# Down product of parts for 36 chunks instead of 15, with some high parts on GpSimd, in a fused attention and SwiGLU kernel

## The chip, the cores and the metric

The kernel runs on one core of one Trainium2 chip. The metric is the device time of one execution in microseconds (us), as the median of several runs. Beside it there is one profiled execution, whose span and instructions the views below come from. The engines are TensorE (PE for its matmuls, PEld for its weight loads), VectorE (DVE), ScalarE (ACT), GpSimd (POOL) and SyncE (SP), which here only issues DMAs.

## The reference

Two stages are computed one after the other. First an attention with sketched polynomial features (4 batches, 4 heads, 1088 tokens, head size 32), then a feed-forward block on its 4352 x 128 result.

```python
def _attn_ref(q, k, v, S1, S2):
    def phi(x):
        a = np.einsum('rd,bhsd->bhsr', S1, x)
        b = np.einsum('rd,bhsd->bhsr', S2, x)
        return np.einsum('bhsi,bhsj->bhsij', a, b).reshape(*x.shape[:-1], r * r)
    q_p, k_p = (phi(q), phi(k))
    kv = np.einsum('bhsf,bhsd->bhfd', k_p, v)
    z = np.sum(k_p, axis=2)
    num = np.einsum('bhsf,bhfd->bhsd', q_p, kv)
    den = np.einsum('bhsf,bhf->bhs', q_p, z)[..., None] + 1e-06
    return num / den

def _moe_ref(x, w_gate, w_val, w_out):
    g = x @ w_gate
    silu = g * (1.0 / (1.0 + np.exp(-g)))
    val = x @ w_val
    return silu * val @ w_out
```

The widths are 128 (model) and 1536 (hidden). The change touches only the last product, `@ w_out`, called the down product here.

## The kernel before

The hidden width is worked on in 12 chunks of 128. The tokens are worked on in ten blocks: three of batch 0 (384, 384 and 320 tokens), which run as soon as their attention is there, and then seven of at most 480 tokens, which form the list `line` (numbered 0 to 6 in this text; 480 tokens each, the last 384). One unit is one chunk of one block. The seven blocks of `line` make 84 units, numbered y = 12 * block + chunk, and a single loop (L1355) runs over them. The attention of batches 1 to 3 is a generator, `attentions`, which that loop advances between the units (`group`, `parts_of`). All of it is one hand-written order: a manual schedule keeps instructions on each engine as they are written.

**A unit.** The gate and value products of the units in `line` are computed from parts in the type float32r: instead of one fp32 product with both factors whole, the factors are cut into a rounded high part, a rest, and a difference of scaled ones, and three float32r matmuls make up the product. `start_unit` issues the matmuls of the differences (L977, two of them, into a pair of PSUM banks) and ScalarE scales them in place (L980). One turn later `finish_unit` adds the other four matmuls (L990, L991), then ScalarE takes the SiLU (L993), and VectorE multiplies it with the value half into a slot of `hbuf` (L998). That releases the pair of PSUM banks; there are three pairs, so a later `start_unit` waits for it.

**The down product.** `down` takes the oldest chunk from the list `todo` once per turn, when over five wait there: the chunk of unit y is used about five turns later. A plain chunk is one fp32 matmul (L1062), which appears in the trace as two passes. For the pairs in `DOWN` the product is made of parts instead: `FINE` holds five chunks (1, 4, 6, 8, 10) and `DOWN` holds them for blocks 3 to 5 of `line`, 15 chunks in all. Such a chunk has three float32r matmuls (L1054, L1056, L1057), two of which sum in a PSUM bank of their own, `acc[i, "p"]`. When the block's last chunk of parts is done, `copy_out` lets ScalarE copy that bank (L1077), and after the block's last chunk `put_together` lets VectorE add both sums (L1083). Plain chunks in such a block use weights scaled beforehand (`scaled`), so that both sums fit.

**The parts.** `cut_hidden` is called at the end of `finish_unit(y)` for a chunk in `DOWN`. It puts off three operations to later turns: the high part h1 by ScalarE behind `finish_unit(y + 1)` (L954), the rest h0 by GpSimd in turn y + 2 (L955), and the scaled difference hd by VectorE in turn y + 3, ahead of that turn's L998 (L958). The results lie in three sets of three buffers, taken in turn (`h_sets`), in memory that the attention has left. `cut_down` makes the same parts of the down weights `wo`, as a generator that the loop advances at y = 24, 26, ..., 36 (L1371): high parts by ScalarE (L923), rests by GpSimd (L926), scaled rests by ScalarE (L931), differences by GpSimd (L934), and the scaled plain weights by ScalarE (L940). `cut_tokens` does the same for the tokens of the next block (L882 on ScalarE, L883 on GpSimd, L887 on VectorE).

```python
        add_to(behind, y + 1, lambda: nc.scalar.activation(h1, h, AF.Copy, scale=CUT))
        add_to(before, y + 2, lambda: nc.gpsimd.tensor_tensor(
            out=h0, in0=h, in1=whole(h1), op=ALU.subtract
        ))
        add_to(before, y + 3, lambda: nc.vector.scalar_tensor_tensor(
            out=hd, in0=whole(h0), scalar=-BETA, in1=whole(h1), op0=ALU.mult, op1=ALU.add
        ))
```

Of the kernel before, what the change touches and what calls it, by code (L numbers as in the profile page):

```python
# [7 lines left out]
FP32 = mybir.dt.float32  # L8
F32R = mybir.dt.float32r
# [3 lines left out]
AF = mybir.ActivationFunctionType  # L13
ALU = mybir.AluOpType
# [5 lines left out]
def kernel(  # L20
# [28 lines left out]
    nc = tc.nc  # L49
    P = nc.NUM_PARTITIONS  # L50
    B, H, S, Dh = q.shape
    R = S1.shape[0]
    D, Dff = moe_w_gate.shape
# [5 lines left out]
    NCH = Dff // P  # L59
# [11 lines left out]
    WB = 480  # L71
# [9 lines left out]
    const = ctx.enter_context(tc.tile_pool(name="const", bufs=1))  # L81
    stage = ctx.enter_context(tc.tile_pool(name="stage", bufs=2))
    apool = ctx.enter_context(tc.tile_pool(name="attn", bufs=1))
# [29 lines left out]
    def bank(tag=None):  # L113

        if tag is not None:
            i = place[tag]
        elif oldest[0]:
            i = min((i for i in used if i not in held), key=used.get)
        else:
            i = place[free_banks[turn[0] % len(free_banks)]]  # L120
            turn[0] += 1
        touch(i)
        return PS[:, i, :]
# [31 lines left out]
    wo = const.tile([P, NCH, D], FP32, name="wo")  # L155
# [32 lines left out]
    def load_next():  # L188
# [36 lines left out]
        out=ident[:], in_=ident[:], pattern=[[-1, P]], base=0, channel_multiplier=1,  # L225
# [90 lines left out]
    late = const.tile([P, NL, BW], FP32, tag="late", name="late", bufs=1)  # L316
# [500 lines left out]
    BETA = 4096.0  # L817
    CUT = 1.0 - 2.0**-13
# [3 lines left out]
    def whole(ap):  # L822
        return ap.bitcast(FP32)
# [17 lines left out]
    def cut_weights(w, lows, engine):  # L841

        rows = [], [], [], []
        sub = dict(op=ALU.subtract)
        for c, (w1, wb, wd) in enumerate(homes(w)):
            src = w[:, 3 * c : 3 * c + 3, :]
            low = lows[c]
            w_parts[id(w), c] = (w1, wb, wd)
            fine = dict(out=wd, in0=whole(w1), in1=whole(wb), **sub), engine.tensor_tensor
            if engine is nc.vector:  # L850
                fine = dict(
                    out=wd, in0=low, scalar=-BETA, in1=whole(w1), op0=ALU.mult, op1=ALU.add
                ), engine.scalar_tensor_tensor
            for row, f, args in zip(
                rows,
                (nc.scalar.activation, engine.tensor_tensor, nc.scalar.activation, fine[1]),
                (
                    dict(out=w1, in_=src, func=AF.Copy, scale=CUT),
                    dict(out=low, in0=src, in1=whole(w1), **sub),
                    dict(out=wb, in_=low, func=AF.Copy, scale=BETA),  # L860
                    fine[0],
                ),
            ):
                row.append((f, args))
        return rows
# [26 lines left out]


    line = list(range(HEAD, len(blocks)))
    FINE, PLAIN = (1, 4, 6, 8, 10), (0, 2, 3, 5, 7, 9, 11)
    DOWN = [(i, j) for i in line[3:6] for j in FINE]
    down_parts = {}
    h_parts = {}
    h_sets = []
    before, behind = {}, {}  # L900

    def add_to(where, y, f):
        where.setdefault(y, []).append(f)

    def now(where, y):
        for f in where.pop(y, ()):
            f()

    def cut_down():

        n = len(FINE)
        parts = const.tile([P, 3, n, D], F32R, tag="late", name="dparts", bufs=1)
        w1, wb, wd = (parts[:, k] for k in range(3))
        scaled = apool.tile([P, len(PLAIN), D], FP32, tag="zs", name="scaled")
        low = [
            apool.tile([P, c, D], FP32, tag=tag, name="low" + tag)[:]
            for tag, c in (("kas", 2), ("kab2", 3))
        ]
        down_parts.update(w1=w1, wb=wb, wd=wd, scaled=scaled)
        cs = slice(0, 2), slice(2, 5)  # L920
        runs = [(0, slice(1, 5, 3)), (2, slice(6, 11, 2))]
        for k, c in runs:
            nc.scalar.activation(w1[:, cs[k > 0]], wo[:, c, :], AF.Copy, scale=CUT)  # L923
        yield
        for (k, c), x in zip(runs, low):
            nc.gpsimd.tensor_tensor(  # L926
                out=x, in0=wo[:, c, :], in1=whole(w1[:, cs[k > 0]]), op=ALU.subtract
            )
            yield
        for c, x in zip(cs, low):  # L930
            nc.scalar.activation(wb[:, c], x, AF.Copy, scale=BETA)  # L931
        yield
        for c in cs:
            nc.gpsimd.tensor_tensor(  # L934
                out=wd[:, c], in0=whole(w1[:, c]), in1=whole(wb[:, c]), op=ALU.subtract
            )
            yield
        for k, c in ((0, slice(0, 1)), (1, slice(2, 4)), (3, slice(5, 12, 2))):
            m = len(range(12)[c])
            nc.scalar.activation(scaled[:, k : k + m, :], wo[:, c, :], AF.Copy, scale=-BETA)  # L940

    def cut_hidden(y, i, j):

        if not h_sets:
            x = []
            for tag in ("kld", "qld", "vld", "kT", "qT"):
                t = const.tile([P, 2, WB], F32R, tag=tag, name="h" + tag, bufs=1)
                x += [t[:, k, :] for k in range(2)]
            h_sets.extend(x[k : k + 3] for k in range(0, 9, 3))
        n = blocks[i][1]  # L950
        h_sets.append(h_sets.pop(0))
        h1, h0, hd = h_parts[i, j] = [x[:, 0:n] for x in h_sets[-1]]
        h = hidden[i, j][:, 0:n]
        add_to(behind, y + 1, lambda: nc.scalar.activation(h1, h, AF.Copy, scale=CUT))  # L954
        add_to(before, y + 2, lambda: nc.gpsimd.tensor_tensor(  # L955
            out=h0, in0=h, in1=whole(h1), op=ALU.subtract
        ))
        add_to(before, y + 3, lambda: nc.vector.scalar_tensor_tensor(  # L958
            out=hd, in0=whole(h0), scalar=-BETA, in1=whole(h1), op0=ALU.mult, op1=ALU.add
        ))  # L960


    room = const.tile([P, 10, BW], FP32, tag="room", name="room", bufs=1)
# [18 lines left out]
    def finish_unit(y):  # L982
        i, j = line[y // NCH], y % NCH
        n = blocks[i][1]
        x1, x0, _ = (x[:, 0:n] for x in x_parts[i])
        ps = sums_of.pop(y)
        now(before, y)
        for k, w in enumerate((wg, wv)):
            w1, wb = (w_parts[id(w), j // 3][t][:, j % 3, :] for t in range(2))
            nc.tensor.matmul(ps[:, k], w1, x1, start=False, stop=False, skip_group_check=True)  # L990
            nc.tensor.matmul(ps[:, k], wb, x0, start=False, stop=True, skip_group_check=True)  # L991
        sg = fpool.tile([P, WB], FP32, tag="sg", name="sg", bufs=5)[:, 0:n]
        nc.scalar.activation(sg, ps[:, 0], AF.Silu, scale=WHOLE)  # L993
        slot_of[i, j] = slots.pop(0)
        hj = slot_of[i, j]
        hidden[i, j] = hj
        todo.append((i, j))
        nc.vector.scalar_tensor_tensor(  # L998
            out=hj[:, 0:n], in0=ps[:, 1], scalar=WHOLE, in1=sg, op0=ALU.mult, op1=ALU.mult
        )  # L1000
        let_go(y)
        now(behind, y)
        if (i, j) in DOWN:
            cut_hidden(y, i, j)
# [36 lines left out]
    def down(y=None):  # L1041
# [3 lines left out]
        if j == 0:  # L1045
            acc[i] = bank("g1" if i == 1 else "g2" if i in line[2::2] else "acc")
        mine = [c for c in range(NCH) if (i, c) in DOWN]
        if mine and j == mine[0]:
# [88 lines left out]
    for h in range(H):  # L1137
# [13 lines left out]
        out=s12[:],  # L1151
        in0=sTv.unsqueeze(1).to_broadcast([P, H, 2, R]),
        in1=own[:].unsqueeze(2).unsqueeze(3).to_broadcast([P, H, 2, R]),
        op=ALU.mult,
# [19 lines left out]
    n = steps[0][1]  # L1174
# [58 lines left out]
    def group():  # L1233
        while ahead[0] != "pe":
            ahead[0] = next(att)
        ahead[0] = next(att, "end")
# [34 lines left out]
    parts = {}  # L1271
# [8 lines left out]
    for z, (i, j) in enumerate(seq):  # L1280
# [16 lines left out]
        if z == 20:  # L1297
# [4 lines left out]
            first, low, second, third = cut_weights(wv, lows, nc.gpsimd)  # L1302
# [48 lines left out]
    oldest[0] = True  # L1351
    hold("acc")
    down_steps = cut_down()
    start_unit(0)
    for y in range(END):  # L1355
        if y in GROUPS:
            group()
        if y in WIDE:
            finish_unit(y)
        if y + 1 < END:  # L1360
            start_unit(y + 1)
        if y not in WIDE:
            finish_unit(y)
        for _ in range(2):

            if len(todo) > min(5 + (todo[0] == (line[1], 0)), END - y + 1):
                down(y)
        parts_of(y < EASY or y % 2 == 0)
        for gen in token_steps.get(y, ()):
            next(gen, None)  # L1370
        if y in range(24, 38, 2):  # L1371
            next(down_steps, None)
    ps = wide("a")[:, 0, 0:D]
    for j in range(NCH):
# [6 lines left out]
    b, x0 = divmod(t0 // 32, NX)  # L1381
# [34 lines left out]
```

## Time and profile before

| What | Value |
|---|---|
| Time, median of 3 runs | 281.87 us (281.57 to 282.72) |
| Time of the profiled execution | 281.56 us |
| Span of the profiled execution | 279.9 us |
| TensorE clock granted | 1.00 |
| VectorE, ScalarE, GpSimd busy | 174.3, 181.5, 76.9 us |
| Plain down products, blocks of `line` without parts (L1062 from hbuf with wo, 128x480) | 72 passes, 565 ns mean |
| Plain down products in blocks with parts (L1062 with scaled) | 42 passes, 564 ns mean |
| Products of parts (L1054, L1056, L1057) | 45 matmuls, 373 to 384 ns |
| h1, h0, hd (L954, L955, L958), 15 of each | 606, 1223 and 649 ns mean |

How to read it: the busy time of a group is the sum of its instructions' durations. TensorE's matmuls overlap in the records (a 480-column matmul lasts 380 ns, but the next starts some 216 ns after it), so what a matmul costs is read from the distance of starts. The same holds to a lesser degree on the other engines, where an instruction's record begins about 0.1 us before the one ahead of it ends. In the lines of the views, an arrow names the tiles written and read, `x2` counts instructions, and a bracket gives how long the engine was idle before and who ended that.

### The profile page before, as it was taken

Reading aid. Unit: us, or ns where it says so; the run is one execution under the profiler, and the core shown is the slowest. Engines: PE = TensorE matmul, PEld = TensorE weight load, DVE = VectorE, ACT = ScalarE, POOL = GpSimd, SP = SyncE. Lnnn points to the kernel's source line nnn. Section 1 sums busy time; section 2 is a strip of 40 time slices with the busy share of each in tenths; the row PEclk is TensorE's granted clock in tenths of the full one; section 3 lists DMA queues with packets and bytes.
Section 4 is the critical chain, followed back from the end, with each engine's and each line's share of the span. In section 5 each row is a group of like instructions: output and inputs, shape, how many; then the busy total and the mean of one; then the engine's idle time right before and its main releaser. Section 6 shows DMA issues by size and latency. Waiting matters only on the chain.

```text
span 279.9 us, 5561 instructions
## 1 busy us (share of the span) xinstructions
PE 273.3 (98%) x2154; PEld 195.5 (70%) x2154; DVE 174.3 (62%) x327; ACT 181.5 (65%) x323; POOL 76.9 (27%) x93
## 2 busy tenths in 40 slices
PE   7899999999999999999999999999999999999995
PEld 6645565666756687777577767757777778778994
DVE  3997987976688863887544565545436444644431
ACT  3468566555511686677457786869788888877860
POOL 3314422179720530160010140013313333131000
PEclk9999999999999999999999999999999999999999
DMA  6573195222041123000200020002000200100011
GB/s 193 164 226 78 49 284 171 82 80 80 20 108 28 27 85 91 2 1 2 36 13 4 0 39 0 0 2 35 1 0 2 35 0 0 23 15 1 9 30 28
DMA packets 26139, 14.30 MB, mean 51 GB/s; under 512 B 19840, under 2 KB 24192, under 8 KB 26112
## 3 DMA queue, kind: packets, MB, share of 16 engines
q1 hardware_dynamic: 25456, 13.84, 19.2%
q8 instruction: 17, 0.28, 0.4%
q10 hardware_dynamic: 656, 0.10, 0.2%
q14 instruction: 10, 0.08, 0.1%
HBM read 11.41 MB, written 2.23 MB: 49 GB/s over the span
## 4 chain that ended last, share of the span: by engine, by line
PE 94%; DVE 2%; DMA 2%; ACT 1%; issue 0%; SPq 0%
PE PS L1062 26%; PE PS L1014 16%; PE PS L990 13%; PE PS L977 13%; PE PS L991 13%; PE PS L783 2%; PE PS L357 2%; PE PS L345 2%; PE PS L391 2%; DMA kld<-in_k_dram 2%; PE PS L1057 1%; PE PS L1054 1%; PE PS L1056 1%; PE PS L1090 1%; PE PS L500 1%; PE PS L448 1%
## 5 line engine op out<-in xcount | busy, mean ns | idle before, releaser
L980 ACT ACTIVATE PS<-PS 128x960 f32<-128x960 f32 (+1 forms) x84 | 78.3, 934 | 37.1 <-PE PS L977 36.6
L998 DVE SCALAR_TENSOR_TENSOR hbuf<-PS,sg 128x480 f32<-128x480 f32 (+1 forms) x84 | 54.0, 643 | 75.2 <-ACT sg L993 74.9
L1062 PE MATMUL PS<-hbuf,wo 128*128 128x480 f32 (+3 forms) x142 | 57.5, 505 | 0.0
L977 PE MATMUL PS<-xd,gphq 128*128 128x480 f32 (+1 forms) x84 | 52.2, 622 | 0.0
L993 ACT ACTIVATE sg<-PS 128x480 f32<-128x480 f32 (+1 forms) x84 | 46.6, 555 | 2.0 <-PE PS L991 1.3
L990 PE MATMUL PS<-x,graw 128*128 128x480 f32 (+1 forms) x84 | 32.1, 382 | 0.6 <-ACT PS L980 0.6
L1062 PEld LDWEIGHTS PS<-hbuf,wo 128*128 128x128 f32 x142 | 26.6, 189 | 8.2 <-issue 0.9
L991 PE MATMUL PS<-x,wb 128*128 128x480 f32 (+1 forms) x84 | 31.6, 376 | 0.0
L977 PE MATMUL PS<-xd,wd 128*128 128x480 f32 (+1 forms) x84 | 31.4, 374 | 0.0
L990 PE MATMUL PS<-x,w 128*128 128x480 f32 (+1 forms) x84 | 31.4, 374 | 0.0
L991 PE MATMUL PS<-x,graw 128*128 128x480 f32 (+1 forms) x84 | 31.3, 372 | 0.0
L1014 PE MATMUL PS<-xT,wg 128*128 128x384 f32 (+1 forms) x72 | 28.7, 480 | 0.0
L1014 PE MATMUL PS<-xT,wv 128*128 128x384 f32 (+1 forms) x72 | 28.0, 470 | 0.2 <-DVE wv L289 0.2
L1018 ACT ACTIVATE sg<-PS 128x384 f32<-128x384 f32 (+1 forms) x30 | 13.9, 466 | 18.7 <-PE PS L1014 17.0
L977 PEld LDWEIGHTS PS<-xd,gphq 128*128 128x128 f32 x84 | 15.8, 188 | 12.5 <-ACT PS L980 9.6
L977 PEld LDWEIGHTS PS<-xd,wd 128*128 128x128 f32 x84 | 15.9, 189 | 12.2 <-issue 9.0
L1062 PE MATMUL PS<-hbuf,scaled 128*128 128x480 f32 x42 | 20.3, 564 | 0.0
L1014 PEld LDWEIGHTS PS<-xT,wv 128*128 128x128 f32 x72 | 13.4, 190 | 8.9 <-DVE hbuf L1029 0.9
L1014 PEld LDWEIGHTS PS<-xT,wg 128*128 128x128 f32 x72 | 12.9, 189 | 9.3 <-issue 1.2
L883 POOL TENSOR_TENSOR x<-xT,x 128x480 fp32r<-128x480 f32 (+1 forms) x6 | 7.1, 1178 | 42.8 <-ACT x L882 42.8
L990 PEld LDWEIGHTS PS<-x,graw 128*128 128x128 f32 x84 | 15.7, 187 | 4.3 <-ACT PS L980 1.6
L990 PEld LDWEIGHTS PS<-x,w 128*128 128x128 f32 x84 | 15.8, 188 | 2.1
(169 smaller groups left out, 409.8 us busy)
## 6 DMA issues: line engine op xcount, KB each, us to landing
kld<-in_k_dram SPq DMA_DIRECT2D x4, 544.0 KB, 4.4
vld<-in_v_dram SPq DMA_DIRECT2D x12, 144.0 KB, 4.6
qld<-in_q_dram SPq DMA_DIRECT2D x3, 544.0 KB, 3.5
raw<-in_moe_w_out_dram SPq DMA_DIRECT2D x4, 384.0 KB, 4.0
raw<-in_moe_w_gate_dram SPq DMA_DIRECT2D x3, 384.0 KB, 3.7
raw<-in_moe_w_val_dram SPq DMA_DIRECT2D x3, 384.0 KB, 3.6
out_dram<-o SPq DMA_DIRECT2D x16, 60.0 KB, 1.9
vld<-in_v_dram SPq DMA_DIRECT2D x4, 112.0 KB, 4.4
```

The costliest lines, as they stand in the source:

```text
L345: nc.tensor.matmul(ps[32 * a : 32 * a + 32, 96 * (c - c0) : 96 * (c - c0) + 96], qT[:, 4 * c + a, :], s123[:, a : a + H, :, :].rearrange(" ...
L357: nc.tensor.matmul(ps[32 * a : 32 * a + 64, 64 * (c - c0) : 64 * (c - c0) + 64], kT[:, c, a : a + 2, :].rearrange("p a t -> p (a t)"), s12 ...
L883: engine.tensor_tensor(out=x0[:, 0:n], in0=x, in1=whole(x1[:, 0:n]), op=ALU.subtract)
L977: nc.tensor.matmul(ps[:, k], w_parts[id(w), j // 3][2][:, j % 3, :], xd, start=True, stop=True)
L980: nc.scalar.activation(ps, ps, AF.Copy, scale=-1.0 / BETA / WHOLE)
L990: nc.tensor.matmul(ps[:, k], w1, x1, start=False, stop=False, skip_group_check=True)
L991: nc.tensor.matmul(ps[:, k], wb, x0, start=False, stop=True, skip_group_check=True)
L993: nc.scalar.activation(sg, ps[:, 0], AF.Silu, scale=WHOLE)
L998: nc.vector.scalar_tensor_tensor(out=hj[:, 0:n], in0=ps[:, 1], scalar=WHOLE, in1=sg, op0=ALU.mult, op1=ALU.mult)
L1014: nc.tensor.matmul(o[:, 0:n], w[:, j, :], xT[:, t0 : t0 + n], start=True, stop=True)
L1018: nc.scalar.activation(sg[:, 0:n], g[:, 0:n], AF.Silu)
L1062: nc.tensor.matmul(acc[i][:, 0:n], w, hidden[i, j][:, 0:n], **sides)
```

## The change

Four things change.

- `FINE` holds the ten chunks 1 to 10, and `DOWN` holds all ten for blocks 3 to 5 and six (2, 4, 6, 8, 9, 10) for block 2: 36 chunks instead of 15. The plain chunks of these blocks are 0 and 11, and in block 2 also 1, 3, 5 and 7.
- `cut_down` cuts ten chunks of weights, in three groups of three, three and four, in a new order of steps at y = 20 to 28, one in each turn. The parts lie in the memory of `room`, the rests in that of `late`.
- `cut_hidden` has six sets of buffers instead of three; the new ones lie in the memory of `late`, after the rests of the weights.
- The high part h1 is made by GpSimd (`tensor_scalar`, a multiplication by `CUT` with float32r output) for every chunk of block 2 and for the odd chunks of blocks 3 to 5, and by ScalarE for the even ones as before.

```diff
-    FINE, PLAIN = (1, 4, 6, 8, 10), (0, 2, 3, 5, 7, 9, 11)
-    DOWN = [(i, j) for i in line[3:6] for j in FINE]
+    FINE, PLAIN = range(1, NCH - 1), (0, 1, 3, 5, 7, NCH - 1)
+    DOWN = [(i, j) for i in line[2:6] for j in FINE if i != line[2] or j not in PLAIN]
...
-        parts = const.tile([P, 3, n, D], F32R, tag="late", name="dparts", bufs=1)
+        parts = const.tile([P, 3, n, D], F32R, tag="room", name="dparts", bufs=1)
...
+        low = const.tile([P, n, D], FP32, tag="late", name="dlow", bufs=1)
...
+        def high(c):
+            nc.scalar.activation(w1[:, c], wo[:, FINE[0] :][:, c], AF.Copy, scale=CUT)
+
+        def left(c):
             nc.gpsimd.tensor_tensor(
+                out=low[:, c], in0=wo[:, FINE[0] :][:, c], in1=whole(w1[:, c]), op=ALU.subtract
             )
+
+        def scale(c):
+            nc.scalar.activation(wb[:, c], low[:, c], AF.Copy, scale=BETA)
+
+        def differ(c):
             nc.gpsimd.tensor_tensor(
                 out=wd[:, c], in0=whole(w1[:, c]), in1=whole(wb[:, c]), op=ALU.subtract
             )
+
+        def other(k, c):
+            m = len(range(NCH)[c])
+            nc.scalar.activation(scaled[:, k : k + m, :], wo[:, c, :], AF.Copy, scale=-BETA)
+
+        a, b, c = slice(0, 3), slice(3, 6), slice(6, n)
+        for step in (
+            [(high, a)], [(left, a), (high, b)], [(left, b), (scale, a)], [(differ, a), (high, c)],
+            [(left, c), (scale, b)], [(differ, b), (scale, c)], [(differ, c), (other, *rest[0])],
+            [(other, *rest[1])], [(other, *rest[2])],
+        ):
+            for f, *args in step:
+                f(*args)
             yield
...
-            h_sets.extend(x[k : k + 3] for k in range(0, 9, 3))
+            t = const.tile([P, 8, WB], F32R, tag="late", name="hlate", bufs=1)
+            x += [t[:, k, :] for k in range(8)]
+            h_sets.extend(x[k : k + 3] for k in range(0, 18, 3))
...
-        add_to(behind, y + 1, lambda: nc.scalar.activation(h1, h, AF.Copy, scale=CUT))
+        if i == line[2] or j % 2:
+            add_to(behind, y + 1, lambda: nc.gpsimd.tensor_scalar(h1, h, CUT, None, op0=ALU.mult))
+        else:
+            add_to(behind, y + 1, lambda: nc.scalar.activation(h1, h, AF.Copy, scale=CUT))
...
-        if y in range(24, 38, 2):
+        if y in range(20, 30):
             next(down_steps, None)
```

More of the change, by code (lines that the diff above doesn't have):

```diff
@@ L911, in cut_down @@
         n = len(FINE)
-        parts = const.tile([P, 3, n, D], F32R, tag="late", name="dparts", bufs=1)
+        parts = const.tile([P, 3, n, D], F32R, tag="room", name="dparts", bufs=1)
         w1, wb, wd = (parts[:, k] for k in range(3))
         scaled = apool.tile([P, len(PLAIN), D], FP32, tag="zs", name="scaled")
[L915 to L918, printed above, removed]
+        low = const.tile([P, n, D], FP32, tag="late", name="dlow", bufs=1)
         down_parts.update(w1=w1, wb=wb, wd=wd, scaled=scaled)
[L920 to L925, printed above, removed]
+        rest = [(0, slice(0, 1)), (1, slice(1, 8, 2)), (5, slice(NCH - 1, NCH))]
+        def high(c):
+            nc.scalar.activation(w1[:, c], wo[:, FINE[0] :][:, c], AF.Copy, scale=CUT)
+        def left(c):
             nc.gpsimd.tensor_tensor(
-                out=x, in0=wo[:, c, :], in1=whole(w1[:, cs[k > 0]]), op=ALU.subtract
+                out=low[:, c], in0=wo[:, FINE[0] :][:, c], in1=whole(w1[:, c]), op=ALU.subtract
             )
[L929 to L933, printed above, removed]
+        def scale(c):
+            nc.scalar.activation(wb[:, c], low[:, c], AF.Copy, scale=BETA)
+        def differ(c):
             nc.gpsimd.tensor_tensor(
@@ L936, in cut_down @@
             )
+        def other(k, c):
[9 more added lines that the diff above has]
+                f(*args)
             yield
-        for k, c in ((0, slice(0, 1)), (1, slice(2, 4)), (3, slice(5, 12, 2))):
-            m = len(range(12)[c])
-            nc.scalar.activation(scaled[:, k : k + m, :], wo[:, c, :], AF.Copy, scale=-BETA)
     def cut_hidden(y, i, j):
```

## The prediction

> **What bounds the kernel now.** First the page: shares and the chain of work that ended last.
>
> ```profile
> PE 273.3 (98%) x2154; PEld 195.5 (70%) x2154; DVE 174.3 (62%) x327; ACT 181.5 (65%) x323; POOL 76.9 (27%) x93
> PE 94%; DVE 2%; DMA 2%; ACT 1%; issue 0%; SPq 0%
> ```
>
> A busy TensorE proves little by itself; that 94% of the chain is TensorE does. Then the windows of the stretch in which blocks 3 to 5 run (window, length, busy us of PE, PEld, DVE, ACT, POOL, then clock and DMA):
>
> ```profile
> 200.00:220.00 20.00, 20.00 (x84) 15.40 (x82) 10.60 (x17) 16.84 (x27) 6.08 (x5) 1.00 0.07 12
> 220.00:240.00 20.00, 20.00 (x84) 15.59 (x83) 9.98 (x16) 16.66 (x27) 5.85 (x5) 1.00 0.01 2
> ```
>
> TensorE has no gap, POOL is idle 70%. So a saving on TensorE is worth its full size until another engine fills. What a unit costs is read from the chain in order of time, by the starts of L977 (once a unit):
>
> ```profile
> 203.79 0.43 PE PS L977 x2
> ...
> 205.11 0.81 PE PS L1062 x2
> ...
> 205.91 0.44 PE PS L977 x2
> ...
> 207.88 0.44 PE PS L977 x2
> ...
> 209.98 0.44 PE PS L977 x2
> ```
>
> A unit with a plain down product takes 205.91 - 203.79 = 2.12 and 209.98 - 207.88 = 2.10 us; one with a product of parts 207.88 - 205.91 = 1.97, and the one ahead of this stretch 203.79 - 201.84 = 1.95. A plain product is two passes (x2, 0.81 us together); the parts are three matmuls, each 0.22 after the one before it.
>
> Last, how GpSimd and VectorE meet. The first two lines are from one stretch of the timeline, the others from another.
>
> ```profile
> 166.17 2.42 POOL L934 TENSOR_TENSOR dparts<-dparts 128x256 fp32r<-128x256 f32 x2 [4.01 <-ACT dparts L931]
> ...
> 166.39 1.33 DVE L380 TENSOR_TENSOR phq<-qab 128x768 f32<-128x768 f32 x1
> ```
> ```profile
> 212.02 1.23 POOL L955 TENSOR_TENSOR hkT<-hbuf,hkT 128x480 fp32r<-128x480 f32 x1
> 212.15 0.66 DVE L998 SCALAR_TENSOR_TENSOR hbuf<-PS,sg 128x480 f32<-128x480 f32 x1 [1.68 <-ACT sg L993]
> ...
> 212.72 1.04 DVE L887 SCALAR_TENSOR_TENSOR xd<-x,x 128x480 fp32r<-128x480 f32 x1
> ...
> 213.69 0.65 DVE L958 SCALAR_TENSOR_TENSOR hqT<-hkT 128x480 fp32r<-128x480 f32 x1
> ```
>
> L887 (both inputs in SBUF) takes 1.04 instead of the 0.65 seen elsewhere and ends at 213.76, 0.51 after POOL's end at 213.25; L998 (one input in PSUM) beside the same POOL instruction keeps its 0.66. At 166.39 L380 takes 1.33 instead of 0.95, and POOL's second L934 takes 1.72 instead of the 1.01 of the equal L926.
>
> **What the Trainium skill says.** SBUF — State Buffer, section "SBUF: two separate sides": VectorE and GpSimd share a port pair under an exclusive lock; a VectorE operation with two SBUF inputs and a GpSimd operation that reads SBUF hold each other off for a whole instruction. The lines above agree: 0.39 us late on VectorE, 0.71 on POOL. GPSIMD Engine Reference, section "Engine selection": one-input operations on GpSimd run at roughly line rate, two-input ones about twice slower than on VectorE. The trace agrees on the second (1.22 against 0.65); of the first it shows only small copies.
>
> **The change part by part.**
>
> TensorE: parts go from 15 to 36 chunks, so 21 plain products leave (21 x 0.81 = 17.0) and 63 matmuls come (63 x 0.2155 = 13.6, the spacing in the timeline): -3.4. By unit times (2.12 - 1.95 = 0.17) it is 21 x 0.17 = -3.6. I take -3.5, all on the path.
>
> ScalarE: high parts by L954 stay 15 (five in each of blocks 3 to 5; block 2's are all on GpSimd). Added: one sum copy of 0.58, and weight cuts over 3328 columns for 2176: from 0.42, 0.53, 0.42, 0.53, 0.31, 0.42, 0.63 to some 4.6, so +1.4. They move from units 24 to 36 to units 20 to 28, near 142 to 160 us. There L980 waits 0.69 us for TensorE in each unit, which takes one insert (0.31 to 0.63) a unit; without that cover each would cost its own length. A pair of units in blocks 3 to 5 needs, by starts, 2 x (0.87 + 0.45) + 0.49 = 3.1 us of ScalarE against TensorE's 2 x 1.945 = 3.89. Cost 0.
>
> VectorE: 21 more L958 at 0.65, and in block 2 one more sum (0.65): +14.3 us, in stretches where it is half idle; its work alone costs 0. It counts through the lock.
>
> GpSimd: 21 more subtractions at 1.22 (1.18 by starts: 210.84 to 212.02), 21 new high parts, and weight cuts for ten chunks instead of five (+3.5 at most, before block 2 needs them). No row shows a high part on POOL. The nearest are
>
> ```profile
> L955 POOL TENSOR_TENSOR hkld<-hbuf,hkld 128x480 fp32r<-128x480 f32 x5 | 6.1, 1224 | 26.6 <-ACT hkld L954 26.6
> ...
> L1181 POOL COPY s<-s 128x64 f32<-128x64 f32 x2 | 0.5, 235 | 0.0
> ...
> L1182 POOL COPY own<-own 128x4 f32<-128x4 f32 x2 | 0.4, 185 | 0.0
> ```
>
> From the copies, 50 ns for 60 columns, 480 columns give an estimate of 0.185 + 476 x 0.00083 = 0.58. Above it is bounded by the two-input 1.22, since it reads half as much. I take 0.65.
>
> The lock: a steady pair of units is two subtractions (2 x 1.18), one high part (0.65), two L958 that hold it for about 0.5 each, and 0.1 between a high part and the subtraction that waits for it: 4.1, less about 0.1 at each blocked start (L934's second ended 0.87 after L380, against 0.96 by starts): 3.9 to 4.1, against TensorE's 3.89. So POOL falls behind by 0 to 0.2 a pair, at most 1.0 over a block's five pairs; units 11 and 0 have no parts and let it catch up (the x0 of the next block, 1.2, fits into such a gap).
>
> What waits behind: L958 of chunk y stands ahead of L998 of y + 3 in VectorE's order, and L998 frees the PSUM pair for the L977 three units on. VectorE idles 1.3 between two L998 without L958 (1.29 and 1.31 at 205.73 and 209.81), so 0.65 is left; L998 ended at 208.51, the next L977's weights came at 209.42, 0.9 more. TensorE stalls only once POOL is 1.55 late. At 1.0 it doesn't. Block 2 adds L380 (0.95) to the lock and has three parts in a row with both operations on POOL (chunks 8, 9, 10): 1.83 + 0.5 + 0.4 = 2.7 a unit against 1.95, late by about 2 at the end; as its high part comes first, L958 has a whole unit more. I put 0.3 for the whole run; bounds 0 and 4.
>
> DMA queues carry the same transfers; only block 2's four stores now follow one more addition, in the middle of the run, cost 0.
>
> Sum against the profiled execution: 281.56 (span 279.9, 1.66 around it) - 3.5 + 0.3 = 278.4. The median shown is 281.87, 0.3 above that execution; 278.5 between the two.
>
> **The rivals.**
>
> (a) POOL's high part is dear: at 1.17 a pair takes 4.5, late by 0.6 a pair, 3.0 a block; 3.0 - 1.55 = 1.4 of stall in each of three blocks, 4.2 less the 3.5: about 282. For it: no such operation is in the trace, and the lock is proved. Against: copies are cheap. A half-way price, 0.95, gives a few tenths of stall a block: 279.5.
>
> (b) Slower: the same port, but with POOL as the full bound of blocks 3 to 5. At a high part of 1.5 (a start-up of its own, or waits at each hand-over) the pair takes 4.85, 0.95 late, 4.75 a block, 3.2 of stall, 9.6 less 3.5: 288. It is slower by over 0.5% from about 1.25 on. Against: it would have to cost more than the two-input subtraction.
>
> (c) ScalarE's cuts hit the busy units around 142 to 147 us, where x1 already made TensorE wait 0.27 for L980: two to three inserts of 0.5 uncovered, 1.0 to 1.5: 279.7.
>
> That the change doesn't do what it says: the new list of instructions has 42 more TensorE rows, which is 21 chunks with three in place of one. Ruled out.
>
> **How the numbers follow.** Forecast 0.68 (277.7 to 279.3), (c) or the half-way price 0.12, (a) 0.12, (b) 0.08. A measurement of this kernel tells about 0.5% (1.4 us) from no change, so faster means under 280.5: 0.68 + 0.12 = 0.80; (a) is the same, 0.12; (b) slower, 0.08. The range reaches down to the lock and the cover costing nothing (277.6) and up through the cheap half of (a), 281.2.
>
> **What would show it.** Units of blocks 3 to 5 at 1.95 in the chain; 108 matmuls of parts; POOL high parts near 0.65 and POOL some 75% busy from 185 to 250 us; L958 often at 0.9 to 1.5 as it meets the lock; idle of TensorE under 0.5 there. I am wrong if the high part exceeds 1.0, if L977 waits for L998, or if TensorE idles for ScalarE's cuts at 142 to 150 us.

## The result and the profile after

The changed kernel takes 282.4 us (median of 20 runs, 281.98 to 283.94), the kernel before 281.68 us (20 runs beside it): ratio 1.0025, 95% interval 1.0014 to 1.0037. It is a quarter of a per cent slower: clear of zero, and within what the prediction called no change. The forecast of 278.5 is missed by 4 us, and the time lies above the top of its range, 281.2. The profiled execution spans 280.5 us, against 279.9.

The page of the kernel after, the same two lines as before:

```profile
PE 272.8 (97%) x2175; PEld 198.7 (71%) x2175; DVE 201.9 (72%) x349; ACT 183.4 (65%) x326; POOL 142.0 (51%) x137
...
PE 89%; DVE 4%; POOL 2%; DMA 1%; issue 1%; ACT 1%; SPq 0%; DVEq 0%
```

GpSimd's busy time almost doubles (76.9 to 142.0 us), and VectorE's grows by 27.6 us (174.3 to 201.9) where its added work had been put at 14.3. The share of TensorE in the chain falls from 94% to 89%; VectorE's grows from 2% to 4%, and GpSimd stands in it with 2%. The windows of blocks 3 to 5 (window, length, busy us of PE, PEld, DVE, ACT, POOL, clock, DMA):

```profile
200.00:220.00 20.00, 19.82 (x87) 15.71 (x85) 15.67 (x20) 16.58 (x26) 17.52 (x13) 1.00 0.00 1
220.00:240.00 20.00, 19.80 (x86) 15.97 (x87) 15.41 (x20) 16.87 (x26) 17.44 (x14) 1.00 0.08 13
```

TensorE was busy 20.00 of 20 us before; now it has gaps. They look small because a matmul's record is longer than its slot and covers the start of a gap. GpSimd is busy 87%, which leaves little to catch up in. The chain of waits, in order of time, shows what a gap is:

```profile
225.88 0.43 PE PS L989 x2
...
227.44 0.66 DVE hbuf L1010
228.14 0.48 PE PS L989
```

(L989 was L977, L1003 was L991, L1010 was L998, L964 and L966 are the high parts on GpSimd and ScalarE, L967 was L955, L970 was L958, L1066 was L1054.) From L989 at 225.88 to the next at 228.14 are 2.26 us instead of 1.95, and the chain passes through L1010: TensorE waited for the product on VectorE that frees the PSUM pair.

The ends of the scaling on ScalarE (L980 before, L992 after), one per unit, give the step of each unit in both traces. Worked out from them, the units of the changed kernel that are late (step in us, and how much further behind the kernel before this unit puts it):

```
block 3 unit 10  2.70  +0.59      block 5 unit 3   2.33  +0.37
block 4 unit 3   2.26  +0.30      block 5 unit 9   2.22  +0.13
block 4 unit 9   2.42  +0.32      block 6 unit 1   2.42  +0.49
block 5 unit 1   2.34  +0.39      block 6 unit 3   2.47  +0.77
```

Their sum is +3.4. In blocks 3 to 5 the other units with a product of parts take 1.93 to 1.99, and all other units together gain 2.5. From -0.19 at the first unit (ahead of the kernel before) the changed kernel goes down to -1.0 in block 3, and ends at +0.68. So the saving on TensorE came, and eight stalls gave it back.

What makes one is seen in the timeline of the kernel after, its first stall:

```profile
191.66 1.22 POOL L967 TENSOR_TENSOR hlate<-hbuf,hqT 128x480 fp32r<-128x480 f32 x1
191.74 1.66 DVE L970 SCALAR_TENSOR_TENSOR hqT<-hkT 128x480 fp32r<-128x480 f32 x1 [0.47 <-POOL hkT L967]
...
193.91 0.61 DVE L1010 SCALAR_TENSOR_TENSOR hbuf<-PS,sg 128x480 f32<-128x480 f32 x1
...
194.76 3.00 POOL L967 TENSOR_TENSOR hlate<-hbuf,hlate 128x480 fp32r<-128x480 f32 x2
195.01 1.68 DVE L970 SCALAR_TENSOR_TENSOR hlate<-hlate,hqT 128x480 fp32r<-128x480 f32 x1
...
196.62 0.64 DVE L1010 SCALAR_TENSOR_TENSOR hbuf<-PS,sg 128x480 f32<-128x480 f32 x1
...
197.31 0.19 PEld L989 LDWEIGHTS PS<-xd,wd 128*128 128x128 f32 x1 [0.90 <-DVE hbuf L1010]
```

The difference L970 waits for the subtraction of its own chunk. At that moment GpSimd's next operation begins (191.66) and the difference comes 0.08 us later (191.74): it takes 1.66 us, its own 0.65 and about 1.0 of the operation ahead of it at the shared port. The next difference, at 195.01, runs into a subtraction that has begun at 194.76, and takes 1.68. L1010 stands behind it on VectorE, comes at 196.62, and L989 waits 0.90 us for it. The groups by form of the same kernel, from 130 us on (count, busy us, mean ns, idle before and what ended it):

```profile
L967 POOL TENSOR_TENSOR hlate<-hbuf,hlate 128x480 fp32r<-128x480 f32 x12 | 15.7, 1328 | 0.5
...
L964 POOL TENSOR_SCALAR hlate<-hbuf 128x480 fp32r<-128x480 f32 x7 | 11.9, 1704 | 2.3 <-DVE hbuf L1010 2.3
...
L970 DVE SCALAR_TENSOR_TENSOR hqT<-hkT 128x480 fp32r<-128x480 f32 x6 | 9.0, 1493 | 2.9 <-POOL hkT L967 2.9
...
L964 POOL TENSOR_SCALAR hqT<-hbuf 128x480 fp32r<-128x480 f32 x1 | 1.4, 1411 | 0.7 <-DVE hbuf L1010 0.7
```

The high part on GpSimd takes 1.40 to 1.42 us in seven cases, and mostly 1.82 where it is queued behind a difference that has the port first (191.74 to 193.40, and the high part from 192.85 to 194.67). The means of the differences hide two kinds. In blocks 4 and 5 those of the odd chunks take 1.66 to 1.68: most of them are released by a subtraction behind which the subtraction of the next chunk is queued already. Those of the even chunks take 0.63 to 0.65. They mostly run while a high part is under way, which does not hold them (at 203.02 a difference of 0.64, with a high part on GpSimd from 201.99 to 203.81). In the kernel before all fifteen took 0.65.

### The profile page after: what moved, and what is told of

It reads as the page before. It is cut to its first block, busy times and chain, and to the rows that moved or that the text cites. A ratio compares the mean times of both kernels' runs of the same rounds, so it can differ in the third digit from the quotient of the medians.

```text
span 280.5 us, 5696 instructions
## 1 busy us (share of the span) xinstructions
PE 272.8 (97%) x2175; PEld 198.7 (71%) x2175; DVE 201.9 (72%) x349; ACT 183.4 (65%) x326; POOL 142.0 (51%) x137
## 4 chain that ended last, share of the span: by engine, by line
PE 89%; DVE 4%; POOL 2%; DMA 1%; issue 1%; ACT 1%; SPq 0%; DVEq 0%
PE PS L1074 20%; PE PS L1026 16%; PE PS L989 13%; PE PS L1002 13%; PE PS L1003 12%; PE PS L1066 2%; PE PS L1069 2%; PE PS L1068 2%; PE PS L783 2%; PE PS L345 2%; PE PS L357 2%; DVE hbuf L1010 2%; PE PS L391 2%; DMA kld<-in_k_dram 1%; PE PS L1102 1%
## 5 line engine op out<-in xcount | busy, mean ns | idle before, releaser
L992 ACT ACTIVATE PS<-PS 128x960 f32<-128x960 f32 (+1 forms) x84 | 78.3, 934 | 35.4 <-PE PS L989 34.8
L1010 DVE SCALAR_TENSOR_TENSOR hbuf<-PS,sg 128x480 f32<-128x480 f32 (+1 forms) x84 | 53.4, 636 | 41.0 <-ACT sg L1005 40.9
L1074 PE MATMUL PS<-hbuf,wo 128*128 128x480 f32 (+3 forms) x118 | 45.9, 492 | 0.0
L989 PE MATMUL PS<-xd,gphq 128*128 128x480 f32 (+1 forms) x84 | 44.8, 534 | 0.0
L989 PE MATMUL PS<-xd,wd 128*128 128x480 f32 (+1 forms) x84 | 32.3, 384 | 1.6 <-DVE hbuf L1010 1.2
L1003 PE MATMUL PS<-x,wb 128*128 128x480 f32 (+1 forms) x84 | 31.6, 376 | 0.0
L1003 PE MATMUL PS<-x,graw 128*128 128x480 f32 (+1 forms) x84 | 31.3, 373 | 0.0
L1074 PEld LDWEIGHTS PS<-hbuf,wo 128*128 128x128 f32 x118 | 22.1, 189 | 7.4 <-issue 0.9
L989 PEld LDWEIGHTS PS<-xd,wd 128*128 128x128 f32 x84 | 15.8, 188 | 13.4 <-issue 5.5
L989 PEld LDWEIGHTS PS<-xd,gphq 128*128 128x128 f32 x84 | 15.8, 188 | 8.8 <-ACT PS L992 5.3
L1003 PEld LDWEIGHTS PS<-x,wb 128*128 128x128 f32 x84 | 15.8, 188 | 2.1
```

Source lines behind the costliest of these rows:

```text
L989: nc.tensor.matmul(ps[:, k], w_parts[id(w), j // 3][2][:, j % 3, :], xd, start=True, stop=True)
L992: nc.scalar.activation(ps, ps, AF.Copy, scale=-1.0 / BETA / WHOLE)
L1010: nc.vector.scalar_tensor_tensor(out=hj[:, 0:n], in0=ps[:, 1], scalar=WHOLE, in1=sg, op0=ALU.mult, op1=ALU.mult)
L1074: nc.tensor.matmul(acc[i][:, 0:n], w, hidden[i, j][:, 0:n], **sides)
```

## The experiments

Two causes offered themselves: the price of the high part on GpSimd (theory A) and the meeting at the shared port (rival B, sharpened to D after the first runs), with VectorE's order as a third (rival C). Ratios are to the kernel before, run on the same chip.

**All high parts of activations on ScalarE.**

```diff
-        if i == line[2] or j % 2:
-            add_to(behind, y + 1, lambda: nc.gpsimd.tensor_scalar(h1, h, CUT, None, op0=ALU.mult))
-        else:
-            add_to(behind, y + 1, lambda: nc.scalar.activation(h1, h, AF.Copy, scale=CUT))
+        add_to(behind, y + 1, lambda: nc.scalar.activation(h1, h, AF.Copy, scale=CUT))
```

> The changed kernel with all 36 high parts of activations on ScalarE and none on GpSimd; everything else as changed. Theory A (the high part on GpSimd, 1.41 us free and up to 1.82 with the lock, makes GpSimd the bound of blocks 3 to 5): the stalls go and the saving on TensorE stays, 21 x 0.16 = 3.4 us, so 278.3 (277.7 to 279.3), no wait of L977's successor for the product on VectorE. Rival B (the shared port: ten subtractions and ten differences a block hold each other off, whoever makes the high part): stalls of 0.3 to 0.7 remain in most pairs, 280.5 to 282.5. ScalarE then needs 2 x 1.32 + 2 x 0.49 = 3.6 of 3.89 us a pair; if it is the bound instead, TensorE waits for the scaling on ScalarE.

279.48 us, ratio 0.9918 (0.9902 to 0.9934). The stalls in blocks 3 to 5 are gone, so the high parts on GpSimd are needed for them. The meeting at the port is not gone: most differences of these blocks take 1.1 to 1.5 us here too. But h0 is ready about 2 us before the turn's SiLU ends (0.0 to 0.5 us before it, for most odd chunks of the changed kernel), and L1010 mostly begins within 0.3 us of it. So it takes both, a late h0 and a lost port. The time is 0.2 above the range of theory A, and ScalarE accounts for that: the timeline of this run, at units 4 and 5 of block 3 (L963 is the high part, L1086 the sum copy, L989 the scaling, L999 was L990):

```profile
187.37 0.59 ACT L963 ACTIVATE hkT<-hbuf 128x480 fp32r<-128x480 f32 x1
187.87 0.56 ACT L1086 ACTIVATE sum<-PS 128x480 f32<-128x480 f32 x1
...
188.31 0.97 ACT L989 ACTIVATE PS<-PS 128x960 f32<-128x960 f32 x1
...
189.34 0.19 PEld L999 LDWEIGHTS PS<-x,graw 128*128 128x128 f32 x1 [0.83 <-ACT PS L989]
```

Two inserts stand ahead of one scaling, and TensorE's next weight load waits 0.83 us. By the steps of the units this run loses 0.48 us against the changed kernel at unit 5 of block 3 (5.84 us instead of 5.37).

**All of them on GpSimd.**

```diff
-        if i == line[2] or j % 2:
-            add_to(behind, y + 1, lambda: nc.gpsimd.tensor_scalar(h1, h, CUT, None, op0=ALU.mult))
-        else:
-            add_to(behind, y + 1, lambda: nc.scalar.activation(h1, h, AF.Copy, scale=CUT))
+        add_to(behind, y + 1, lambda: nc.gpsimd.tensor_scalar(h1, h, CUT, None, op0=ALU.mult))
```

> The changed kernel with all 36 high parts of activations on GpSimd: the suspected cost doubled in blocks 3 to 5. Theory A: GpSimd needs 10 x (1.18 + 1.41) + 1.2 + some 5 us of lock = 32 us a block against 23.6, so some 8 us a block more than TensorE needs, 24 in all: about 302, not under 292. Rival B: the lock matters only by the number of reads, 15 more short ones: 283 to 287.

294.87 us, ratio 1.0479 (1.0449 to 1.0508): fifteen high parts more cost 12.5 us over the changed kernel. GpSimd is the bound of these blocks:

```profile
185.00:260.00 75.00, 67.90 (x327) 50.20 (x299) 49.70 (x65) 47.85 (x70) 68.85 (x53) 1.00 0.06 11
```
```profile
197.40 1.41 POOL L963 TENSOR_SCALAR hlate<-hbuf 128x480 fp32r<-128x480 f32 x1
...
197.47 1.03 DVE L967 SCALAR_TENSOR_TENSOR hlate<-hlate 128x480 fp32r<-128x480 f32 x1 [1.08 <-POOL hlate L964]
```

It is busy 68.85 of 75 us, the steady units take 2.67 to 2.69 us, which is one high part and one subtraction (1.49 + 1.18 by starts). Rival B is out by 8 us, and theory A's sum was too dear by 7: it added some 5 us of lock a block, while most high parts (1.41) and subtractions (1.22) keep their length here. The last two lines (L963 is the high part, L967 the difference) show the difference behind a high part that began 0.07 us earlier: it takes 1.03, so it waited 0.39 us and ended 0.31 before the high part did. So a high part held the port for a part of its time only; "for a whole instruction", which the prediction took over, fits the subtraction and not this operation.

**The difference one place later on VectorE.** L1010 of a turn then stands ahead of the difference of three turns before.

```diff
-        add_to(before, y + 3, lambda: nc.vector.scalar_tensor_tensor(
+        add_to(behind, y + 3, lambda: nc.vector.scalar_tensor_tensor(
             out=hd, in0=whole(h0), scalar=-BETA, in1=whole(h1), op0=ALU.mult, op1=ALU.add
```

> The changed kernel with the scaled difference on VectorE (hd) put behind the product of turn y + 3 instead of ahead of it, nothing else. Theory A (GpSimd has too much work in a block): the stalls move but stay, 281 to 283. Rival C (GpSimd's work fits, and only the order on VectorE, hd ahead of the product that frees the PSUM pair, turns its lateness into stalls): 278.3 to 279.5.

279.67 us, ratio 0.9926 (0.9908 to 0.9944), 0.2 above rival C's range. GpSimd does all that it does in the changed kernel, and 2.7 us come back. So GpSimd's work fits into blocks 3 to 5, and it was the place of the difference that turned its lateness into stalls: rival C, and theory A falls as it stood. One stall is left, in the last block, where the units are shorter, and there TensorE waits for the difference itself. The waits of this run from 245 to 265 us:

```profile
PEld PS L1066 <- DVE hlate L970: 0.9, 1, 0.9
```

**The high part as a product of two tensors.** The column `cutter` holds CUT.

```diff
-            add_to(behind, y + 1, lambda: nc.gpsimd.tensor_scalar(h1, h, CUT, None, op0=ALU.mult))
+            add_to(behind, y + 1, lambda: nc.gpsimd.tensor_tensor(
+                out=h1, in0=h, in1=cutter[:].to_broadcast([P, n]), op=ALU.mult
+            ))
```

> The changed kernel with the same high parts on GpSimd, but as a product of two tensors, the second a constant column spread over the row. Theory A: free of the lock it takes about 1.2 us as the subtraction does instead of 1.41, so 0.2 a pair less, 3 us less of lateness over three blocks: 280 to 281.5. Rival B: no change, 282.4.

281.71 us, ratio 1.0001 (0.9992 to 1.001): 0.7 less than the changed kernel, between both expectations and not decisive. The high part takes 0.99 us where nothing disturbs it and 1.28 to 1.36 on average. One stall of 1.7 us at unit 10 of block 3 takes much of what the cheaper operation brings.

**A copy in place of the multiplication.** The factor CUT is left out.

```diff
-            add_to(behind, y + 1, lambda: nc.gpsimd.tensor_scalar(h1, h, CUT, None, op0=ALU.mult))
+            add_to(behind, y + 1, lambda: nc.gpsimd.tensor_copy(h1, h))
```

> The changed kernel with a plain rounding copy on GpSimd in place of the multiplication by CUT; the factor CUT of the high part is left out for those chunks. If the one-input copy takes the 0.58 to 0.65 us that the prediction's sum had put in, the sum itself is tested. Theory A (only the price was wrong): stalls go, 278.3 to 279.3. Theory D (each difference on VectorE is ready at the very moment at which GpSimd has begun its next operation, so it waits one whole operation; what counts is whether GpSimd has a backlog): with 0.6 in place of 1.4 most subtractions of odd chunks have nothing behind them, so also 278.5 to 279.5, with L958's successor at 0.65 to 1.2 instead of 1.0 to 1.5. If the copy costs 1.4 too: 282.4, and the price belongs to one-input operations at large.

280.24 us, ratio 0.9953 (0.9939 to 0.9967), above what both theories had expected. Its groups by form and its waits from 185 to 260 us:

```profile
L964 POOL CAST hlate<-hbuf 128x480 fp32r<-128x480 f32 x7 | 6.2, 891 | 4.5 <-DVE hbuf L1010 4.5
...
L964 POOL CAST hqld<-hbuf 128x480 fp32r<-128x480 f32 x1 | 0.6, 584 | 0.2 <-DVE hbuf L1010 0.2
```
```profile
PEld PS L989 <- DVE hbuf L1010: 1.6, 2, 1.4
```

The copy takes 0.584 us where nothing disturbs it, the prediction's 0.58, and 0.89 to 0.97 on average; a multiplication by a constant is another operation at 2.4 times the price. Here the prediction's own price is in place, and the time is still 1.7 us above its 278.5: one stall, at unit 10 of block 3 (3.26 us in place of 1.97), from two differences in a row that lose the port. So the price was one of two errors; it is worth 2.2 us here.

**Only the high parts on GpSimd, in the kernel before.**

```diff
-        add_to(behind, y + 1, lambda: nc.scalar.activation(h1, h, AF.Copy, scale=CUT))
+        add_to(behind, y + 1, lambda: nc.gpsimd.tensor_scalar(h1, h, CUT, None, op0=ALU.mult))
```

> The kernel before with its 15 high parts on GpSimd instead of ScalarE: that part of the change alone. GpSimd then has some 5 x (1.4 + 1.2) + 1.2 = 14 us in a block of 24.4. Theory A and D: no backlog, so no stall, 281.4 to 282.2, and the price of the high part free of the lock is seen, about 1.41. If the high part on GpSimd does harm by itself (its wait for the product on VectorE): 283 or more.

281.64 us, ratio 1.0001 (0.9986 to 1.0016): no change, as expected. The high part takes 1.41 us in six cases and about 1.75 in nine, mostly where it starts behind a difference, and costs nothing: GpSimd has no backlog there, and fourteen of the fifteen differences keep their 0.65 (one takes 1.03).

**High parts of blocks 3 to 5 on ScalarE, of block 2 on GpSimd, difference later.**

```diff
-        if i == line[2] or j % 2:
+        if i == line[2]:
...
-        add_to(before, y + 3, lambda: nc.vector.scalar_tensor_tensor(
+        add_to(behind, y + 3, lambda: nc.vector.scalar_tensor_tensor(
```

> The changed kernel with the high parts of blocks 3 to 5 on ScalarE, those of block 2 left on GpSimd, and hd behind the product of turn y + 3. The inserts on ScalarE that made TensorE wait 0.7 and 0.5 us in the run with all high parts there were in block 2 and at its end. Theory D: all of the saving on TensorE comes out, 278.0 to 278.9. If it stays at 279.5 as the two single remedies did, something else takes the rest.

279.25 us, ratio 0.9919 (0.9894 to 0.9943). The median is 0.2 to 0.4 below that of either remedy alone, but by the ratios (0.9918 and 0.9926 there) no gain is shown, and the time is short of the expectation: unit 5 of block 3 took 5.85 us where the changed kernel needs 5.37. It is the place on ScalarE shown above, with the high parts that the changed kernel has on GpSimd.

**The same with nine chunks of parts in block 2.**

```diff
-    DOWN = [(i, j) for i in line[2:6] for j in FINE if i != line[2] or j not in PLAIN]
+    DOWN = [(i, j) for i in line[2:6] for j in FINE if i != line[2] or j > 1]
```

> As the mixed one with hd behind, and block 2 with nine chunks of parts (2 to 10) instead of six, all high parts of it on GpSimd. TensorE saves 3 x 0.16 = 0.5 us more: 277.6 to 278.5. Against it: nine units in a row at 1.41 + 1.18 us and more on GpSimd are 2.6 to 3.1 against 1.96, late by 6 to 9 us over block 2, more than the two turns that hd now has, so by theory A and D it is slower than the mixed one, 280 to 283.

282.87 us, ratio 1.004 (1.0027 to 1.0052): the objection was right. Units 0 and 4 of block 3 take 3.64 and 3.25 us, and TensorE waits there for VectorE: for L1010, for L887 and for differences that come too late. Three chunks more on TensorE's cheap side cost 3.6 us against the mixed kernel, and each of them needs a high part and a subtraction on GpSimd.

**A difference with one SBUF input, and its control.** The question left open by the run with the difference later was whether it is the port or the plain wait for h0 that delays L1010. In both kernels the matmul with wd reads h1 instead of hd, so the factor hd is left out, and the operation on VectorE writes to a scratch tile. In the first it is a block transpose of h0, in the control it is the difference. The first diff makes the control out of the changed kernel (its sets of buffers also lose hd), the second makes the run with the transpose out of the control.

```diff
         add_to(before, y + 3, lambda: nc.vector.scalar_tensor_tensor(
-            out=hd, in0=whole(h0), scalar=-BETA, in1=whole(h1), op0=ALU.mult, op1=ALU.add
+            out=scrap[0][:, j % 2, 0:n], in0=whole(h0), scalar=-BETA, in1=whole(h1), op0=ALU.mult, op1=ALU.add
         ))
...
-            nc.tensor.matmul(acc[i][:, 0:n], wd, hd, **sides)
+            nc.tensor.matmul(acc[i][:, 0:n], wd, h1, **sides)
```
```diff
-        add_to(before, y + 3, lambda: nc.vector.scalar_tensor_tensor(
-            out=scrap[0][:, j % 2, 0:n], in0=whole(h0), scalar=-BETA, in1=whole(h1), op0=ALU.mult, op1=ALU.add
-        ))
+        add_to(before, y + 3, lambda: nc.vector.transpose(
+            out=scrap[0][:, j % 2, 0:n].rearrange("p (x t) -> p x t", t=32),
+            in_=whole(h0).rearrange("p (x t) -> p x t", t=32),
+        ))
```

> The changed kernel, GpSimd's work untouched, with the two-input difference on VectorE replaced by a block transpose of h0 (one SBUF input, 0.67 us in the trace of before, still waiting for h0), written to a scratch tile; the matmul with wd reads h1 in its place, so the factor hd is left out. Theory D (the difference loses the shared port to GpSimd's next operation): the operation takes 0.67 in every turn instead of 1.0 to 1.5, subtractions stay at 1.22, L1010 is no longer late, stalls go: 278.2 to 279.5. Rival E (not the port but the plain wait for a late h0 ahead of the product): the stalls stay, 281.5 to 282.6.

> The control for the run with the one-input operation: the same scratch tile, and the matmul with wd reads h1 too (the factor hd is left out), but the operation on VectorE stays the two-input difference. Both theories: as the changed kernel, 282.0 to 282.8. If it is faster by over 0.5 us, the buffers or TensorE's wait for hd had a part in it.

278.55 us, ratio 0.9885 (0.9854 to 0.9917), and for the control 282.36 us, 1.0017 (1.0005 to 1.0029), the changed kernel's time. One operation with the same wait, place and length, but with one SBUF input, takes all stalls away. Of the run with the transpose, groups by form, two lines of the timeline (L972 is the transpose, L1013 was L1010) and the window of blocks 3 to 5:

```profile
L966 POOL TENSOR_SCALAR hlate<-hbuf 128x480 fp32r<-128x480 f32 x7 | 9.9, 1411 | 2.6 <-DVE hbuf L1013 2.6
...
L972 DVE STREAM_TRANSPOSE scrap<-hkT 128x480 f32<-128x480 f32 x6 | 4.1, 675 | 1.1 <-POOL hkT L969 1.1
```
```profile
191.80 0.68 DVE L972 STREAM_TRANSPOSE scrap<-hkT 128x480 f32<-128x480 f32 x1 [0.47 <-POOL hkT L969]
...
192.97 0.62 DVE L1013 SCALAR_TENSOR_TENSOR hbuf<-PS,sg 128x480 f32<-128x480 f32 x1
```
```profile
185.00:260.00 75.00, 75.00 (x393) 62.58 (x360) 48.58 (x78) 63.26 (x99) 57.85 (x46) 1.00 0.07 11
```

and of the control, the group of the same tile:

```profile
L972 DVE SCALAR_TENSOR_TENSOR scrap<-hkT 128x480 f32<-128x480 f32 x6 | 9.0, 1496 | 2.8 <-POOL hkT L969 2.8
```

The transpose takes 0.675 us where the difference takes 1.496, GpSimd's high part falls from 1.70 to 1.41, and GpSimd from some 63 busy us of 75 (63.16 in the changed kernel) to 57.85. The time alone does not separate theory D from the plain wait (rival E), because GpSimd, which no longer waits at the port, is also less late. The turn shown does: the transpose at 191.80 and the difference at 191.74 begin after the same wait of 0.47 us for h0, and the product follows 1.17 us after the transpose (192.97) and 2.17 after the difference (193.91). So the port delays the product, as theory D has it. In the changed kernel all eight stalls follow a product that begins 1.5 to 2.0 us after its SiLU's end, and none follows one at 1.3 or less. The latest h0 ends 0.2 us after the SiLU; an estimate for the plain wait behind it, with a difference of 0.65, is a product 0.9 us late, which would not have stalled TensorE.

**The two repairs of what was left.** First as the mixed kernel, with block 3's odd high parts on GpSimd; second as the changed kernel with the difference later and two high parts at the end of block 5 on ScalarE. Each diff shows the high parts alone, the first against the mixed kernel, the second against the changed one.

```diff
-        if i == line[2]:
+        if i == line[2] or i == line[3] and j % 2:
```
```diff
-        if i == line[2] or j % 2:
+        if i == line[2] or j % 2 and (i != line[5] or j < 6):
```

> As the mixed one with hd behind (279.25), but the odd chunks of block 3 have their high parts on GpSimd as in the changed kernel, since ScalarE's insert at the end of block 2 cost 0.5 us there (unit 5 of block 3 took 5.85 instead of 5.37). If so, 278.7 (278.3 to 279.0); if ScalarE was not the cause, 279.2 again.

> As the changed kernel with hd behind (279.67), but the chunks 7 and 9 of block 5 have their high parts on ScalarE: there TensorE waited 0.9 us for hd at unit 4 of the last block, where the units are shorter. If that wait goes, 278.8 (278.4 to 279.2); if GpSimd's lateness comes from before, 279.6 again.

278.67 us, ratio 0.988 (0.9849 to 0.9911), and 278.76 us, 0.9885 (0.9857 to 0.9913). Both computations are complete, and both beat the kernel before by some 2.9 us. The window of the first has no gap left on TensorE:

```profile
185.00:260.00 75.00, 75.00 (x384) 62.56 (x360) 61.20 (x78) 67.48 (x109) 46.77 (x36) 1.00 0.07 11
```

Unit 5 of block 3 is back at 5.36 us. The gain is most of the 3.5 us that the prediction had worked out for TensorE, with VectorE's order and ScalarE's turns arranged for it.

## Why the prediction was wrong

- **TensorE's term was right.** Units with parts take 1.93 to 1.99 us (1.95 was said), and where the stalls are removed the run is 3.0 us faster than before, of 3.5 on record. TensorE's wait for ScalarE at the weight cuts evens out: unit 5 of block 2 takes 2.35 and the next 1.90.
- **"I take 0.65" for the high part on GpSimd, with the two-input 1.22 as the upper bound: failed.** It is 1.41 free and mostly 1.82 where it waits for a difference. The estimate from the copies was exact for a copy (0.584), but the operation is a multiplication, and the reason given for the upper bound (it reads half as much) does not hold for it. Rival (a) named the danger and priced it at 1.17.
- **"Two L958 that hold it for about 0.5 each": failed, in two ways.** On GpSimd's side it counted too much: the high part gives up about 0.41 once a pair, and the pair takes 4.3 us by starts (199.63 to 203.89, and 13.03 for three pairs from 215.84), the 0.41 and the true price together. On VectorE's side it counted nothing. A difference is released by the very subtraction behind which GpSimd's next subtraction is already queued, and so loses the port for that operation: 1.66 us in place of 0.64, once a pair while there is a backlog.
- **"TensorE stalls only once POOL is 1.55 late": failed with it, and this is the step that made the stalls.** That slack was added up from L958's free time and L998's, as if L958 kept its length, although the prediction expected L958 "often at 0.9 to 1.5". The 1.02 that an odd chunk's difference loses leaves about 0.5 of the 1.55. An estimate from these numbers: a pair of 4.3 against TensorE's 3.9 is 0.4 late, 2.0 over a block's five pairs, 1.5 more than the slack, 4.5 in three blocks; the late units add up to 3.4. (Part of the gap: only products over 1.3 us late stalled TensorE, where the prediction had 0.9.)
- **What each of the two is worth.** With the right price in place (the copy) the time was 280.24. With price and lock left as they were and only the order changed it was 279.67, and with the port taken out and the wrong price left in (the transpose) 278.55. The gains of 2.2, 2.7 and 3.8 us do not add up, since each removes in part the same stalls.
- **ScalarE at no cost: right for the changed kernel.** It is wrong with all high parts on ScalarE: unit 5 of block 3 loses 0.48 us.
- **Rivals.** The time is that of (a), 282, and the mechanism is half of (a) and (b): the price was above the 1.25 from which (b) was to decide, but gave 282.4 and not 288. Both rivals counted two holds of 0.5 a pair on GpSimd; (b)'s pair of 4.85 is 0.95 late, the measured 4.3 only 0.4. That (a)'s number came out is in part luck: it had 1.17 for a high part of 1.41, and the two holds made up for it. With the high parts of blocks 3 to 5 doubled GpSimd was the bound, as (b) has it: 294.87.

What stays open: why a stall comes at unit 10 of block 3 in the changed kernel, the control and the runs with the two-tensor product and the copy, while the later ones differ from kernel to kernel. At that stall in the changed kernel two more operations of VectorE, the transpose of block 2's result (193.32) and L887 (194.46), fall between two differences of 1.66 and 1.68, which may be the reason; no run was made on that. Why a multiplication by a constant is so dear on GpSimd is open too.

## What to carry to other kernels

When work goes to GpSimd beside a VectorE operation with two SBUF inputs, look at what releases that operation: if it is a GpSimd instruction with another one queued behind it, add the time for which that one holds the port (here 1.02 us for a subtraction, 0.39 for a high part), and keep it out of the way of whatever on VectorE frees a buffer for the bound engine; one place later in the order was worth 2.7 us here. A price for an engine is a price for one operation on it: a copy, a product with a spread column and a product with a constant cost 0.58, 0.99 and 1.41 us for the same 128 x 480 values. And when a change leaves the time where it was, line both traces up unit by unit: the gain and the stalls that ate it stand side by side there.

## What the runs showed of the hardware that was not expected

- On GpSimd, a multiplication by a constant with float32r output took 1.40 to 1.42 us for 128 x 480 values where nothing disturbed it, longer than the subtraction of two tensors (1.21 to 1.25) and than the product with a spread column (0.98 to 0.99), though it reads one tensor.
- A GpSimd subtraction that was already queued began before the VectorE difference that was waiting for the one ahead of it (191.66 against 191.74), and the difference took 1.66 us in place of 0.64.
- A GpSimd multiplication by a constant held the difference for less than its own length: 0.39 us where it began just ahead of it (197.40 against 197.47), nothing where it was well under way (203.02).
- A block transpose of an SBUF tile on VectorE kept its length (0.64 to 0.68 us) beside a GpSimd that was busy 77% of the time (57.85 of 75 us).
